# First spectral stage with both column halves behind one left factor, and the sums of a and b formed where they are read

## The chip, the cores and the metric

The kernel runs on one core of a Trainium2 chip. The metric is the device time of one execution in microseconds; the median of three runs before the change is 3003.86 us (2996.85 to 3006.36). One further execution was profiled; its rows are the ones quoted below.

## The reference, cut to what matters

Two independent results stand side by side in the output: attention with 32 heads of 32 columns and one shared key and value head (A), and the real part of a two-dimensional Fourier transform written as products of matrices (B). All arrays are float32.

```python
# A: x is 2048 x 1024, wq 1024 x 1024, wk and wv 1024 x 32, wo 1024 x 1024
q = (x @ wq) in 32 heads of 32 columns;  k = x @ wk;  v = x @ wv
p = softmax(q k^T / sqrt(32));  o = p v;  outA = concat(o) @ wo

# B: x is 2048 x 1024, dft_hid 1024 x 1024, dft_seq 2048 x 2048
a = x @ dft_hid_re^T
b = x @ dft_hid_im^T
outB = dft_seq_re @ a - dft_seq_im @ b

out = concat([outA, outB], axis=-1)      # 2048 x 2048
```

## The kernel before

Every product of matrices that is not part of the attention proper is split in precision: an operand is rounded to a high part, the rest is a low part, and three matmuls (high with high, high with low, low with high) make one product of 128 x 128 by 128 x 512. Such matmuls are called fills here, and their running number is the fill position. They are cut into groups that each fill one 128 x 512 bank (`psb`): a group has one or two left items (`mh`, `ml`: 128 x 512, four blocks of weights) and four or eight right items (`rh`, `rl`: 128 x 512). The order of the groups is a list: first those for k, v and q, then `stage1` (112 groups of 12 fills), then `stage2` (112 groups of 24 fills), then the output projection of A.

The attention runs through the whole kernel in 1024 steps. A step has two matmuls of scores (`pss`), a row maximum on DVE (`nm`), the exponentials on ACT, two matmuls of transposed scores (`pst`) with exponentials into the tile `p`, and every eight steps the matmuls of p and v. `level` hands out the fills in proportion, some five to a step, so that PE alternates between both kinds of work and a stage of the fill list always goes with the same share of attention steps. All five engines keep the order of the program.

How an item gets ready is a line with four steps (`Line`): load, combine, high part, low part, each at a lead in fills ahead of the item's due position; 40, 40, 14 and 8 for right items, 52, 36, 27 and 21 for left items (lines 256 and 257). All DMAs are issued by SP. Combining adds or subtracts several loaded sources on POOL (`comb`, line 210), the high part is a cast on DVE, the low part a subtraction on DVE. A finished left item can be stored and fetched again (`save`, `pre`, `fetch`). The prepared right items sit in 14 buffers, left items in 4.

After a group its `post` runs. If a partial result is to be added, a tile `y` was loaded ahead of time (`load_y`, at most six at once, from 24 fills ahead of the group's end), DVE adds the bank to it, and `store` issues the DMA 9 fills (`BEHIND`) later. Also 9 fills later the six tiles' count is given back (`yused`), and the next `y` may be loaded.

`stage1` forms a and b, both of 2048 x 1024, from x and the two hidden matrices by a scheme of seven products (p1, p2, p6, p7, p5, p3, p4 in this order) instead of eight. The column halves are a pair of real and imaginary blocks (n = 0) and the crosswise pair (n = 1). For each half, for each of the seven products, for each of eight row blocks k there is one group. Partial sums go to memory as `t` and `u2` to `u4`. For n = 0 the left item is made from `xbT`, and its high and low parts are stored in `xb_d`; for n = 1 they are fetched from there. `stage2` multiplies with the sequence matrices (`cT`), again in seven products, whose right operands are single blocks of a and b or sums and differences of two of them. These five sums are formed in `stage1`: where a block is finished whose partner is already in memory, the partner is loaded as one more `y`, POOL adds (`gp.tensor_add` and `gp.tensor_sub` in the `post` of `stage1`), and the sum is stored under the name `r`; single blocks that are needed alone are stored too. `stage2` then loads each right item as one tensor (`right_of`).

Lines that matter: `NR0, NM0, NY` 124, `load_r` 179, `comb` 210, `load_y` 251, `add` with the due positions 262, `take` with `yused` 351 to 373, `stage1` 441, `stage2` 518, `expo` 688, `pv` 698, and the pool `pp` of five tiles `p`, each for two steps. At the start, 28 right items are loaded at once into the not yet used tiles `p` and `h`.

Of the kernel before, what the change touches and what calls it, by code (L numbers as in the profile page):

```python
# [16 lines left out]
P = 128  # L17
# [3 lines left out]
DH = 32  # L21
# [55 lines left out]
class Group:  # L77


    def __init__(self, left, right, post, rows=P, ys=()):  # L80
        self.left, self.right, self.post, self.rows, self.ys = left, right, post, rows, ys
        self.n = 3 * len(right)


@with_exitstack
def tile_kernel(ctx: ExitStack, tc, xT, wq, wkv, wo, xbT, wT, cT, out):
# [19 lines left out]
    xb_d = [[[dram.tile([P, 4, P], F32, name=f"xb_{f}_{k}_{a}") for a in range(2)] for k in range(8)] for f in range(7)]  # L106
# [155 lines left out]
    def add(gs):  # L262

        for g in gs:
            i0 = g.at = end[0]
            end[0] += g.n
            if groups and g.right is not groups[-1].right:
# [83 lines left out]
    def take(n):  # L351
        for _ in range(n):
            if cur["group"] >= len(groups):
                return
            g = groups[cur["group"]]
            j = pos["fill"] - g.at
            if j == 0:
                cur["ps"] = bank("psb", True)
            if j % 3 == 0:
                RL.force(g.right[j // 3])  # L360
            if j % 12 == 0:
                ML.force(g.left[j // 12])
# [12 lines left out]
            run_later()  # L375

# [58 lines left out]
        return Group(left, xs, post)  # L435


    NAMES = {nt: [dram.tile([P, W], F32, name=f"r{i}_{s}") for s in range(NC)] for i, (_, nt, _) in enumerate(PRODUCTS)}
    singles = {k[0]: t for k, t in NAMES.items() if len(k) == 1}

    def stage1():
        done = []
        for n, cols in enumerate((((0, 0), (1, 1)), ((1, 0), (0, 1)))):
            for f, (name, lt, rt, outs) in enumerate(STAGE1):
                keeps = any(t[0] == name for p in STAGE1 for t in p[1] + p[2])

                def x_src(t, k):
                    if isinstance(t[0], str):
                        return (lambda: have(("xr", k), xr_d[k]), t[1])
                    return (lambda: xbT[t[0] * 8 + k, :, t[1] * 4:t[1] * 4 + 4], t[2])  # L450

                def w_src(t, c):
                    if isinstance(t[0], str):
                        return (lambda n=n: have(("wr", n, c), wr_d[n][c]), t[1])
                    r, e = cols[t[0]]
                    return (lambda: wT[r, e, t[1] * 4 + c], t[2])

                R = [Item([w_src(t, c) for t in rt], raw=(wr_d[n][c], ("wr", n, c)) if keeps else None) for c in range(4)]
                for k in range(8):
                    if n:  # L460
                        left = [Item(None, pre=lambda f=f, k=k: have(("xb", f, k), xb_d[f][k]))]
                    else:
                        left = [Item([x_src(t, k) for t in lt], save=(*xb_d[f][k], ("xb", f, k)), raw=(xr_d[k], ("xr", k)) if keeps else None)]
                    ys, plan = [], []
                    for frm, sg, to in outs:
                        it = None
                        if frm is not None:
                            it = Item([(lambda frm=frm, n=n, k=k: have((n, frm, k), u_d[n, frm][k]), 1)])
                            ys.append(it)
                        more = []  # L470
                        if not isinstance(to, str):
                            me = cols[to[1]]
                            s = to[0] * 8 + k
                            for key in NAMES:
                                if len(key) == 2 and me in key:
                                    o = key[0] if key[1] == me else key[1]
                                    if (o, s) in done:
                                        yo = Item([(lambda o=o, s=s: right_of((o,), s), 1)])
                                        ys.append(yo)
                                        more.append((key, yo))  # L480
                            done.append((me, s))
                        plan.append((it, sg, to, more))

                    def post(ps, plan=plan, n=n, k=k, cols=cols):
                        for it, sg, to, more in plan:
# [6 lines left out]
                            if isinstance(to, str):  # L492
                                store(u_d[n, to][k], o, (n, to, k))
                                continue
                            me, s = cols[to[1]], to[0] * 8 + k
# [12 lines left out]
    hs = {}  # L508

    def have(key, ap):  # L510
        assert key in ready, key
        return ap

    def right_of(k, s):
        assert (k, s) in ready
        return NAMES[k][s]

    def stage2():
        seen, total = {}, {}
# [168 lines left out]
    def expo(n):  # L688
        u, r = divmod(n, SU)
        c, hp_ = divmod(r, 2)  # L690
        if hp_ == 0:
            pt[u, c] = pp.tile([P, 4, W], F32, name="p")
        ps = ps_t.tile([P, 2, W], F32, name="pst")
        for a in range(2):
            te.matmul(ps[:, a], kst[:, c * P:(c + 1) * P], qst[u][:, 2 * hp_ + a], start=True, stop=True)
        act.activation(pt[u, c][:, 2 * hp_:2 * hp_ + 2], ps, AF.Exp)

    def pv(u, k):

# [1 line left out]
        ps = bank("psb")  # L701
        for c in range(4 * k, 4 * k + 4):
            for h in range(4):
                te.matmul(ps[h * DH:(h + 1) * DH], v[:, c], pt[u, c][:, h], start=c == 4 * k, stop=c == 4 * k + 3)
        if k == 0:
            ov[u] = onp.tile([P, W], F32, name="ov")
            dve.tensor_copy(ov[u], ps)
# [38 lines left out]
                lse_4(u)  # L746


    room = [(lambda t=t, k=k: t[:, k]) for t in [pp.tile([P, 4, W], F32, name="p") for _ in range(5)] for k in range(4)]
# [109 lines left out]
```

## Time and profile before

| | |
|---|---|
| median of three runs | 3003.86 us (2996.85 to 3006.36) |
| the profiled execution | 2989.74 us, its span 2988.0 us |
| granted TensorE clock, mean | 0.985 |
| PE busy | 2847.3 us, 13904 matmuls |
| DVE busy | 2130.9 us |
| ACT busy | 2246.3 us |
| POOL busy | 584.2 us, 422 instructions |
| DMA | 552.16 MB |

All work is recorded at line 66, since one helper issues every instruction; the rows are told apart by the names of the tiles, output before the arrow and inputs behind it. A stage is found by its tensors: the DMAs of `in_xbT_dram` run from 319.2 to 737.5 us, the first store of `t` starts at 365.3 us, those of `xb` are fetched from 763.7 to 1168.3 us, and the first DMA of `in_cT_dram` (second stage) starts at 1157.0 us. The first spectral stage thus lies between some 355 and 1185 us, the second between 1185 and 2640 us.

### The profile page before, as it was taken

The numbers are of one execution on the slowest core, as the hardware profiler recorded it, in microseconds if no ns is written. First come the engines' busy times: TensorE is split into PE (matmuls) and PEld (weight loads), VectorE is DVE, ScalarE is ACT, GpSimd is POOL, SyncE is SP. The second block draws the span as 40 slices with busy tenths as digits, with TensorE's granted clock in tenths as the row PEclk, the third lists the DMA queues.
The fourth block names the chain that finished last, engine by engine and source line by source line (L and its number), as shares of the span: only waits on it lengthen the run. The fifth ranks groups of instructions, "written<-read, shape, count | busy, mean of one in ns | idle before, by whom it ended". The sixth has DMA issues, their size and how long they took to land.

```text
span 2988.0 us, 40244 instructions
## 1 busy us (share of the span) xinstructions
PE 2847.3 (95%) x13904; PEld 1928.3 (65%) x13904; DVE 2130.9 (71%) x2801; ACT 2246.3 (75%) x3286; POOL 584.2 (20%) x422
## 2 busy tenths in 40 slices
PE   7999998979989888999999999999999999999999
PEld 5767665655656555666666666666666666666656
DVE  6866688867667656778788787788888787865510
ACT  4688887766768666888888887878778788888841
POOL 0000014322141233322221012243232220110000
PEclk9999999989999998999999999999999999999999
DMA  8855579888877788445453244464453442454445
GB/s 292 296 180 159 173 256 312 297 261 264 268 250 254 256 267 279 136 135 166 121 168 121 82 148 132 149 198 141 134 163 116 136 131 75 156 152 138 124 145 162
DMA packets 354892, 552.16 MB, mean 185 GB/s; under 512 B 37760, under 2 KB 102784, under 8 KB 354688
## 3 DMA queue, kind: packets, MB, share of 16 engines
q1 hardware_dynamic: 354688, 549.60, 57.8%
q8 instruction: 109, 1.79, 0.2%
q14 instruction: 95, 0.78, 0.1%
HBM read 393.48 MB, written 154.93 MB: 184 GB/s over the span
## 4 chain that ended last, share of the span: by engine, by line
PE 56%; DVE 7%; DMA 6%; ACT 3%; issue 3%; SPq 1%; POOL 1%; DVEq 0%; ACTq 0%; POOLq 0%
PE psb L66 35%; PE pst L66 11%; PE pss L66 10%; DVE nm L66 3%; DMA r<-y 2%; ACT p L66 2%; ACT pss L66 1%; DMA y<-u 1%; SPq L66 1%; DVE ml L66 1%; DVE rl L66 1%; DVE ov L66 1%; DVE mh L66 1%; POOL m L66 1%; DMA y<-r 0%
## 5 line engine op out<-in xcount | busy, mean ns | idle before, releaser
L66 DVE TENSOR_REDUCE nm<-pss 128x1 f32<-128x1024 f32 x1024 | 1248.5, 1221 | 240.5 <-PE pss L66 237.1
L66 ACT ACTIVATE p<-pst 128x1024 f32<-128x1024 f32 x1024 | 1053.3, 1029 | 387.3 <-PE pst L66 380.8
L66 ACT ACTIVATE pss<-pss,nm 128x1024 f32<-128x1024 f32 x1024 | 1118.1, 1092 | 251.8 <-DVE nm L66 236.7
L66 PE MATMUL psb<-rh,mh 128*128 128x512 f32 (+1 forms) x1852 | 734.5, 397 | 22.5 <-DVE y L66 11.6
L66 PE MATMUL psb<-rh,ml 128*128 128x512 f32 (+1 forms) x1852 | 733.8, 396 | 0.1
L66 PE MATMUL psb<-rl,mh 128*128 128x512 f32 (+1 forms) x1852 | 733.4, 396 | 0.3 <-DVE rl L66 0.3
L66 PE MATMUL pss<-kst,qst 128*128 128x512 f32 x2048 | 665.1, 406 | 55.1 <-ACT pss L66 50.2
L66 PE MATMUL pst<-qst,kst 128*128 128x512 f32 x2048 | 670.0, 408 | 26.6 <-ACT p L66 25.4
L66 PEld LDWEIGHTS pss<-kst,qst 128*128 128x128 f32 x2048 | 371.4, 189 | 258.3 <-issue 92.5
L66 PE MATMUL psb<-p,v 128*32 128x512 f32 x4096 | 476.6, 607 | 23.4 <-DVE y L66 23.3
L66 PEld LDWEIGHTS pst<-qst,kst 128*128 128x128 f32 x2048 | 365.9, 189 | 181.1 <-ACT p L66 107.5
L66 PEld LDWEIGHTS psb<-rh,mh 128*128 128x128 f32 (+1 forms) x1852 | 349.2, 189 | 110.5 <-DVE y L66 13.7
L66 PEld LDWEIGHTS psb<-rl,mh 128*128 128x128 f32 (+1 forms) x1852 | 349.5, 189 | 85.2 <-DVE rl L66 1.8
L66 PEld LDWEIGHTS psb<-rh,ml 128*128 128x128 f32 (+1 forms) x1852 | 349.7, 189 | 84.6 <-issue 0.8
L66 POOL TENSOR_TENSOR m<-m,m 128x512 f32<-128x512 f32 x192 | 264.2, 1382 | 517.5 <-DMA m<-in_cT_dram 379.7
L66 PEld LDWEIGHTS psb<-p,v 128*32 128x32 f32 x4096 | 121.7, 111 | 309.5 <-issue 270.9
L66 DVE TENSOR_TENSOR ov<-ov,psb 128x512 f32<-128x512 f32 x96 | 66.0, 687 | 281.1 <-PE psb L66 281.1
L66 DVE TENSOR_TENSOR ml<-m,mh 128x512 fp32r<-128x512 f32 (+1 forms) x298 | 229.5, 770 | 3.5 <-ACT mh L66 3.1
L66 POOL TENSOR_TENSOR y<-y,h 128x512 f32<-128x512 f32 x64 | 89.9, 1415 | 650.1 <-DVE h L66 575.0
L66 ACT ACTIVATION_READ_ACCUMULATOR pss<-pss,nm 128x1 f32 x1024 | 212.8, 208 | 0.0
L66 DVE CAST mh<-m 128x512 fp32r<-128x512 f32 x291 | 152.3, 523 | 46.6 <-POOL m L66 39.5
L66 DVE TENSOR_TENSOR rl<-r,rh 128x512 fp32r<-128x512 f32 x220 | 176.7, 804 | 4.2 <-ACT rh L66 3.5
(64 smaller groups left out, 837.2 us busy)
## 6 DMA issues: line engine op xcount, KB each, us to landing
m<-in_cT_dram SPq DMA_DIRECT2D x384, 256.0 KB, 3.5
r<-y SPq DMA_DIRECT2D x112, 256.0 KB, 5.2
r<-r SPq DMA_DIRECT2D x112, 256.0 KB, 4.3
y<-y SPq DMA_DIRECT2D x96, 256.0 KB, 4.1
m<-in_xbT_dram SPq DMA_DIRECT2D x80, 256.0 KB, 4.2
y<-u SPq DMA_DIRECT2D x80, 256.0 KB, 3.6
y<-r SPq DMA_DIRECT2D x80, 256.0 KB, 3.3
qst<-qh SPq DMA_DIRECT2D x64, 256.0 KB, 5.7
```

The source lines that it names most:

```text
L66: return lambda *a, **k: self.tc.keep_in_program_order(f(*a, **k))
```

## The change

In `stage1` the loop over the halves n becomes the innermost: a group for n = 0 and the one for n = 1 follow each other with the same left item, and both halves' eight right items are held together. The left item is neither stored nor fetched, and `xb_d` is gone. The blocks of a and b are stored as they are, 64 of them, in `s_d`; no partner is loaded and no sum is made. In `stage2` a right item with two sources loads both, and the add or subtraction is the combine step of its line. For this the second source of a right item gets a tile of its own (two buffers `r1`, where it had one of five tiles `h`), and the tiles `p` become nine of half the size instead of five, so that at the start 26 right items are loaded at once. The due positions of right items are spread over both halves' eight. The count of `y` tiles is given back 18 fills after a group instead of 9.

```diff
         self.n = 3 * len(right)
+
+        self.set, self.first = part or ([right], 0)
...
-            if n == 0:
-                it.t.append(r0p.tile([P, W], F32, name="r0"))
+            if n < 2:
+                it.t.append(r0p.tile([P, W], F32, name=f"r{n}", bufs=NR0 - n))
...
-                    it.due = min(it.need, p0 + (i0 - p0) * (c + 1) // len(g.right))
+                    it.due = min(it.need, p0 + (i0 - p0) * (g.first + c + 1) // (len(g.set) * len(g.right)))
...
-                    soon(lambda n=len(g.ys): yused.__setitem__(0, yused[0] + n))
+                    at(pos["fill"] + 2 * BEHIND, lambda n=len(g.ys): yused.__setitem__(0, yused[0] + n))
...
-        for n, cols in enumerate((((0, 0), (1, 1)), ((1, 0), (0, 1)))):
-            for f, (name, lt, rt, outs) in enumerate(STAGE1):
+        for f, (name, lt, rt, outs) in enumerate(STAGE1):
...
-                R = [Item([w_src(t, c) for t in rt], raw=(wr_d[n][c], ("wr", n, c)) if keeps else None) for c in range(4)]
-                for k in range(8):
-                    if n:
-                        left = [Item(None, pre=lambda f=f, k=k: have(("xb", f, k), xb_d[f][k]))]
-                    else:
-                        left = [Item([x_src(t, k) for t in lt], save=(*xb_d[f][k], ("xb", f, k)), raw=(xr_d[k], ("xr", k)) if keeps else None)]
+            R = [[Item([w_src(t, n, c) for t in rt], raw=(wr_d[n][c], ("wr", n, c)) if keeps else None) for c in range(4)]
+                 for n in range(2)]
+            for k in range(8):
+                left = [Item([x_src(t, k) for t in lt], raw=(xr_d[k], ("xr", k)) if keeps else None)]
+                for n in range(2):
...
-                            if me in singles:
-                                store(singles[me][s], o, ((me,), s))
-                            for key, yo in more:
-                                if key != SUB:
-                                    gp.tensor_add(yo.y, yo.y, o)
-                                elif me == key[0]:
-                                    gp.tensor_sub(yo.y, o, yo.y)
-                                else:
-                                    gp.tensor_sub(yo.y, yo.y, o)
-                                store(NAMES[key][s], yo.y, (key, s))
-                    yield Group(left, R, post, ys=ys)
+                            store(to, o, key)
+                    yield Group(left, R[n], post, ys=ys, part=(R, 4 * n))
...
-                R = [Item([(lambda s=s, nt=nt: right_of(tuple(nt), s), 1)]) for s in range(half * 8, half * 8 + 8)]
+                R = [Item([(lambda s=s, k=k: have((k, s), s_d[k][s]), -1 if nt == SUB and i else 1) for i, k in enumerate(nt)])
+                     for s in range(half * 8, half * 8 + 8)]
...
-    pp = pool(ctx, "pp", 5)
+    pp = pool(ctx, "pp", 9)
...
-        if hp_ == 0:
-            pt[u, c] = pp.tile([P, 4, W], F32, name="p")
+        pt[u, c, hp_] = pp.tile([P, 2, W], F32, name="p")
```

Two places of the order show what moves. The first is the DMA order of SP in the first spectral stage, in product p5, whose groups need two partial sums each. Before, in the half n = 1 (`y` from `u` is a partial sum, `y` from `r` a partner block, `r_…<-y` and `u_…<-y` are stores, `mh` and `ml` from `xb` the left item fetched back):

```order
L66 DMA mh<-xb_7_0_271 128x512
L66 DMA ml<-xb_7_1_272 128x512
L66 DMA u_1_3_380<-y_9401 128x512
L66 DMA r_11_505<-y_9454 128x512
L66 DMA r_11_537<-y_9456 128x512
L66 DMA y_9537<-r_12_522 128x512
L66 DMA y_9539<-r_12_490 128x512
L66 DMA y_9541<-u_1_5_366 128x512
L66 DMA y_9543<-u_1_5_374 128x512
```

And the same product after the change (`m` are the sources of a new left item, which serves two groups; `s_…<-y` stores a finished block):

```order
L66 DMA y_7953<-u_0_5_222 128x512
L66 DMA y_7955<-u_0_5_230 128x512
L66 DMA m_7958<-in_xbT_dram 128x512
L66 DMA m_7960<-in_xbT_dram 128x512
L66 DMA u_0_4_237<-y_7824 128x512
L66 DMA s_12_410<-y_7826 128x512
L66 DMA oh_121<-oh 128x512
L66 DMA ol_125<-ol 128x512
L66 DMA y_8005<-u_1_5_254 128x512
L66 DMA y_8007<-u_1_5_262 128x512
```

Before, a group of p5 has three stores and four loads of `y`, and the loads stand directly behind the stores; now it has two of each, and no `xb` stands between them.

The second place is POOL's order in the fourth product of the second stage, second half, where both a left item with two sources and two sums `y` are formed per group (`h` is the finished product). Before:

```order
L66 TENSOR_TENSOR m_17502<-m_17502,m_17504 128x512
L66 TENSOR_TENSOR y_17517<-y_17517,h_16678 128x512
L66 TENSOR_TENSOR y_17519<-y_17519,h_16678 128x512
L66 TENSOR_TENSOR m_17553<-m_17553,m_17555 128x512
L66 TENSOR_TENSOR m_17601<-m_17601,m_17603 128x512
L66 TENSOR_TENSOR y_17625<-y_17625,h_16802 128x512
L66 TENSOR_TENSOR y_17627<-y_17627,h_16802 128x512
```

After (`r` is the sum of two stored blocks for the next right operand):

```order
L66 TENSOR_TENSOR r_17200<-r_17200,r_17202 128x512
L66 TENSOR_TENSOR m_17150<-m_17150,m_17152 128x512
L66 TENSOR_TENSOR y_17165<-y_17165,h_16300 128x512
L66 TENSOR_TENSOR y_17167<-y_17167,h_16300 128x512
L66 TENSOR_TENSOR m_17205<-m_17205,m_17207 128x512
L66 TENSOR_TENSOR r_17332<-r_17332,r_17334 128x512
L66 TENSOR_TENSOR m_17254<-m_17254,m_17256 128x512
```

One add of `r` per group has come in, and it stands ahead of an add of `m` whose sources SP loads earlier (the numbers rise in the order of the loads: `m_17150` before `r_17200`).

More of the change, by code (lines that the diff above doesn't have):

```diff
@@ L77, with __init__ @@
 class Group:
-    def __init__(self, left, right, post, rows=P, ys=()):
+    def __init__(self, left, right, post, rows=P, ys=(), part=None):
         self.left, self.right, self.post, self.rows, self.ys = left, right, post, rows, ys
         self.n = 3 * len(right)
+        self.set, self.first = part or ([right], 0)
 @with_exitstack
@@ L105, in tile_kernel @@
     wq_d = [[[dram.tile([P, 4, P], F32, name=f"wq_{g}_{q}_{a}") for a in range(2)] for q in range(2)] for g in range(NG)]
-    xb_d = [[[dram.tile([P, 4, P], F32, name=f"xb_{f}_{k}_{a}") for a in range(2)] for k in range(8)] for f in range(7)]
     xr_d = [dram.tile([P, 4, P], F32, name=f"xr_{k}") for k in range(8)]
@@ L266, in add @@
             end[0] += g.n
-            if groups and g.right is not groups[-1].right:
+            if groups and g.set[0] is not groups[-1].set[0]:
                 prev["set"] = prev["this"]
@@ L435, in q_group @@
         return Group(left, xs, post)
-    NAMES = {nt: [dram.tile([P, W], F32, name=f"r{i}_{s}") for s in range(NC)] for i, (_, nt, _) in enumerate(PRODUCTS)}
-    singles = {k[0]: t for k, t in NAMES.items() if len(k) == 1}
+    s_d = {(r, e): [dram.tile([P, W], F32, name=f"s{r}{e}_{s}") for s in range(NC)] for r in range(2) for e in range(2)}
+    COLS = (((0, 0), (1, 1)), ((1, 0), (0, 1)))
     def stage1():
-        done = []
-        for n, cols in enumerate((((0, 0), (1, 1)), ((1, 0), (0, 1)))):
-            for f, (name, lt, rt, outs) in enumerate(STAGE1):
[L445 to L456, printed above, removed]
-                R = [Item([w_src(t, c) for t in rt], raw=(wr_d[n][c], ("wr", n, c)) if keeps else None) for c in range(4)]
-                for k in range(8):
-                    if n:
-                        left = [Item(None, pre=lambda f=f, k=k: have(("xb", f, k), xb_d[f][k]))]
-                    else:
-                        left = [Item([x_src(t, k) for t in lt], save=(*xb_d[f][k], ("xb", f, k)), raw=(xr_d[k], ("xr", k)) if keeps else None)]
@@ new lines, in stage1, with x_src, w_src @@
+        for f, (name, lt, rt, outs) in enumerate(STAGE1):
+            keeps = any(t[0] == name for p in STAGE1 for t in p[1] + p[2])
+            def x_src(t, k):
+                if isinstance(t[0], str):
+                    return (lambda: have(("xr", k), xr_d[k]), t[1])
+                return (lambda: xbT[t[0] * 8 + k, :, t[1] * 4:t[1] * 4 + 4], t[2])
+            def w_src(t, n, c):
+                if isinstance(t[0], str):
+                    return (lambda: have(("wr", n, c), wr_d[n][c]), t[1])
+                r, e = COLS[n][t[0]]
+                return (lambda: wT[r, e, t[1] * 4 + c], t[2])
+            R = [[Item([w_src(t, n, c) for t in rt], raw=(wr_d[n][c], ("wr", n, c)) if keeps else None) for c in range(4)]
[3 more added lines that the diff above has]
+                for n in range(2):
@@ L469, in stage1, with post @@
                             ys.append(it)
[L470 to L485, printed above, removed]
+                        if isinstance(to, str):
+                            plan.append((it, sg, u_d[n, to][k], (n, to, k)))
+                        else:
+                            me, s = COLS[n][to[1]], to[0] * 8 + k
+                            plan.append((it, sg, s_d[me][s], (me, s)))
+                    def post(ps, plan=plan):
+                        for it, sg, to, key in plan:
                             if it is None:
@@ L491, in post @@
                                 (dve.tensor_add if sg > 0 else dve.tensor_sub)(o, o, ps)
[L492 to L495, printed above, removed]
-                            if me in singles:
-                                store(singles[me][s], o, ((me,), s))
-                            for key, yo in more:
-                                if key != SUB:
-                                    gp.tensor_add(yo.y, yo.y, o)
-                                elif me == key[0]:
-                                    gp.tensor_sub(yo.y, o, yo.y)
-                                else:
-                                    gp.tensor_sub(yo.y, yo.y, o)
-                                store(NAMES[key][s], yo.y, (key, s))
-                    yield Group(left, R, post, ys=ys)
+                            store(to, o, key)
+                    yield Group(left, R[n], post, ys=ys, part=(R, 4 * n))
     hs = {}
@@ L512, in have @@
         return ap
-    def right_of(k, s):
-        assert (k, s) in ready
-        return NAMES[k][s]
     def stage2():
@@ L695, in expo @@
             te.matmul(ps[:, a], kst[:, c * P:(c + 1) * P], qst[u][:, 2 * hp_ + a], start=True, stop=True)
-        act.activation(pt[u, c][:, 2 * hp_:2 * hp_ + 2], ps, AF.Exp)
+        act.activation(pt[u, c, hp_], ps, AF.Exp)
     def pv(u, k):
@@ L703, in pv @@
             for h in range(4):
-                te.matmul(ps[h * DH:(h + 1) * DH], v[:, c], pt[u, c][:, h], start=c == 4 * k, stop=c == 4 * k + 3)
+                te.matmul(ps[h * DH:(h + 1) * DH], v[:, c], pt[u, c, h // 2][:, h % 2], start=c == 4 * k, stop=c == 4 * k + 3)
         if k == 0:
@@ L746, in score_step @@
                 lse_4(u)
-    room = [(lambda t=t, k=k: t[:, k]) for t in [pp.tile([P, 4, W], F32, name="p") for _ in range(5)] for k in range(4)]
+    room = [(lambda t=t, k=k: t[:, k]) for t in [pp.tile([P, 2, W], F32, name="p") for _ in range(9)] for k in range(2)]
     room += [(lambda t=t: t) for t in [hp.tile([P, W], F32, name=f"h{k}") for k in range(8)]]
```

## The prediction

> **What bounds the kernel now.** I read the page first, then cut the span into stages, then asked in the worst stage who waits for whom.
>
> ```profile
> PE   7999998979989888999999999999999999999999
> POOL 0000014322141233322221012243232220110000
> DMA  8855579888877788445453244464453442454445
> ```
>
> PE is the busiest engine, and nearly all of its holes lie in slices 7 to 16, where DMA is busy 70 to 90% of the time. The table by stage puts a size to it (columns: PE, PE weight loads, DVE, ACT, POOL busy with counts; granted clock; DMA share; GB/s).
>
> ```profile
> 150.00:355.00 205.00, 203.18 (x1011) 141.62 (x1010) 136.41 (x165) 173.80 (x259) 3.61 (x2) 1.00 0.51 164
> 355.00:1185.00 830.00, 745.93 (x3552) 489.84 (x3554) 583.97 (x759) 587.76 (x857) 229.98 (x166) 0.96 0.82 269
> 1185.00:2640.00 1455.00, 1425.96 (x7137) 967.05 (x7130) 1167.07 (x1553) 1185.63 (x1732) 339.34 (x242) 1.00 0.45 139
> ```
>
> The rows are the q products, the first spectral stage and the second. Fills and attention come in the same proportion in all three, so time per matmul compares them: 205/1011 = 0.2028 us, 830/3552 = 0.2337 us, 1455/7137 = 0.2039 us. At the second stage's rate the first would take 3552 x 0.2039 = 724 us, **106 us less**; at the rate of the q products 720 us, 110 us less. The 106 us have two parts. PE idles 84.1 us instead of 14.5 (29.04 x 3552/7137): 69.6 us. And its busy time per matmul is 0.2100 us instead of 0.1998, with the granted clock at 0.96 instead of 1.00: 36.3 us.
>
> ```profile
> by line: PE psb L66 19.9%; DMA r<-y 7.0%; PE pst L66 6.1%; PE pss L66 5.6%; DMA y<-u 4.9%; SPq L66 3.3%; issue 2.7%; DMA y<-r 1.8%; DVE nm L66 1.4%; ACT p L66 1.2%; DVE y L66 1.2%; DMA y<-t 1.1%; ACT pss L66 0.7%; POOL y L66 0.7%; DMA qst<-
> ...
> DVE y L66 <- DMA y<-u: 47.4, 16, 7.3
> DVE mh L66 <- POOL m L66: 29.4, 9, 8.4
> ...
> DVE y L66 <- DMA y<-t: 8.8, 3, 4.7
> ...
> SPq L66 <- DMA r<-y: 86.1, 71, 5.3
> SPq L66 <- DMA u<-y: 64.8, 21, 6.5
> ```
>
> These are the chain and the waits of that stage alone (355 to 1185 us; total us, times, longest). The chain passes through stores `r<-y`, loads `y<-u`, `y<-r`, `y<-t` and SP's own time for 7.0 + 4.9 + 1.8 + 1.1 + 3.3 = 18.1% of 830 us, some 150 us. DVE, which keeps its order, waits 47.4 + 8.8 us for partial sums and 29.4 us for left items that POOL has not yet combined: 85.6 us, about PE's 84.1 us of idleness. While it waits, the row maxima behind it wait too, then ACT's exponentials, then PE. And the partial sums are late because SP stands 86.1 + 64.8 us before loads whose `y` tile is still being stored: the load is placed directly behind the store.
>
> **The change, part by part.**
>
> ```profile
> r<-y SPq DMA_DIRECT2D x112, 256.0 KB, 5.2
> r<-r SPq DMA_DIRECT2D x112, 256.0 KB, 4.3
> ...
> y<-u SPq DMA_DIRECT2D x80, 256.0 KB, 3.6
> y<-r SPq DMA_DIRECT2D x80, 256.0 KB, 3.3
> ...
> xb<-mh SPq DMA_DIRECT2D x56, 256.0 KB, 3.9
> xb<-ml SPq DMA_DIRECT2D x56, 256.0 KB, 4.2
> mh<-xb SPq DMA_DIRECT2D x56, 256.0 KB, 4.7
> ml<-xb SPq DMA_DIRECT2D x56, 256.0 KB, 5.0
> ```
>
> *Transfers of the first stage.* All 224 transfers of `xb` go. Of 112 stores `r<-y` 64 remain as plain blocks, and the 80 loads `y<-r` go: 224 + 48 + 80 = 352 transfers of 0.262 MB, 92 MB. The stage moves 269 GB/s x 830 us = 223 MB; with 131 MB in some 735 us it would move 178 GB/s, close to the 164 GB/s of the q products, where PE idles 1.8 of 205 us.
>
> *The y tiles.* In p5 for n = 1 a group needs four `y`, so six tiles cover one and a half groups of 12 fills, and the load sits right behind a store that takes 5.2 us to land. Afterwards no group needs more than two; six tiles cover three groups, 36 fills, and the count comes back after 18. In p5 that leaves the load 18 fills or more ahead of its use; at 830 us for 1344 fills (112 groups of 12) a fill takes 0.62 us, so 11 us, against a landing of 3.6 us. The same delay for the second stage costs nothing: its groups have 24 fills, so 24 + 18 fills with two `y` hold at most four tiles of six.
>
> *POOL and the left items.* The 80 adds of partners leave the first stage, where they stood in POOL's order ahead of left sums and waited for DVE. A new left item is due every 24 fills instead of every 12 in the first half and none in the second, so its loads, casts and subtractions spread evenly; DVE's total stays.
>
> ```profile
> L66 DVE TENSOR_TENSOR y<-y,psb 128x512 f32<-128x512 f32 x111 | 74.6, 680 | 79.6 <-DMA y<-u 47.4 <-PE pst L66 9.4 <-DMA y<-t 8.8
> ...
> L66 DVE TENSOR_TENSOR ml<-m,mh 128x512 fp32r<-128x512 f32 x55 | 46.1, 839 | 0.0
> L66 DVE CAST mh<-m 128x512 fp32r<-128x512 f32 x56 | 28.9, 516 | 30.8 <-POOL m L66 29.4 <-DMA m<-in_xbT_dram 1.2
> ```
>
> Per 24 fills DVE then has one left item less than in the second stage (0.52 + 0.84 us) and two additions of `y` more (2 x 0.68 us): the same load, at which it is busy 80% there (1167.07/1455) and PE idles 2.0%.
>
> I take **nine tenths of 106 us, 95 us**. The missing tenth is for the p3, p4, p5 and p6 groups, where two or three sources per left item and right sums still meet two `y` per group.
>
> *The second stage.* It gains 80 loads `r<-s` (21 MB on 202 MB) and 80 adds on POOL with the price of the old ones, 1.37 us:
>
> ```profile
> L66 POOL TENSOR_TENSOR y<-y,y 128x512 f32<-128x512 f32 x80 | 108.6, 1373 | 206.7 <-DVE y L66 127.8 <-DMA y<-r 61.8 <-DMA rb<-r 9.7
> ...
> 1650.00:1725.00 75.00, 74.30 (x371) 51.29 (x364) 57.27 (x82) 62.78 (x94) 0.00 (x0) 1.00 0.22 71
> 1950.00:2025.00 75.00, 70.54 (x344) 47.75 (x343) 67.47 (x81) 58.28 (x85) 33.00 (x24) 1.00 0.65 202
> 2025.00:2100.00 75.00, 73.98 (x379) 49.53 (x378) 58.23 (x81) 61.56 (x92) 20.13 (x15) 1.00 0.46 132
> ```
>
> POOL has room (339 + 110 of 1455 us). But PE's busy time falls from 74.30 us in a stretch without POOL to 70.54 us with 24 of its instructions: 0.157 us each. With 15 of them it falls by 0.32 us, 0.02 each. The new adds come on top of dense phases (five per group in the fourth product, where four stood), so I take the dear end, 80 x 0.157 = **12.5 us**; the cheap end is 80 x 0.02 = 1.7 us, and the costliest is the third rival below. There is no reason for a gain.
>
> Why POOL's density costs DVE time, the rows of the same two stretches show:
>
> ```profile
> L66 DVE TENSOR_TENSOR ml<-m,mh 128x512 fp32r<-128x512 f32 x12 | 8.2, 683 | 0.0
> ...
> L66 DVE TENSOR_TENSOR ml<-m,mh 128x512 fp32r<-128x512 f32 x12 | 11.2, 930 | 0.0
> ```
>
> The subtraction takes 683 ns with POOL still and 930 ns beside it. The Trainium skill ("SBUF — State Buffer", Who interferes with whom) says that DVE with two inputs in SBUF and GpSimd lock each other out for a whole instruction instead of sharing. The trace shows far less than a whole lockout on average, because most instructions do not meet.
>
> *Tiles p and the start.* Nine half tiles hold what the next step of p and v reads (eight) and one being written. No wait comes with it: the matmuls `pst` of the step that reuses a tile stand behind those of p and v on PE, so ACT waits for `pst` anyway.
>
> ```profile
> ACT p L66 <- PE pst L66: 380.8, 277, 5.3
> ...
> p<-in_xT_dram SPq DMA_DIRECT2D x20, 256.0 KB, 5.4
> ```
>
> Two of the 28 early loads come later; hidden behind the first k and v products I cost them at nothing, and fully exposed they would be 2 x 5.4 = 11 us.
>
> *Sum.* -95 + 12.5 = -83 us, so the profiled execution's 2989.74 us would be 2907 us. The runs' median is 14 us above that execution; I carry the difference over unchanged: 3003.86 - 83 = **2921 us**.
>
> **The rivals.**
>
> 1. *The waits only halve.* SP still stands before loads behind stores, and the left items of p6 to p4 still meet right sums on POOL. For it: 28.2 of DVE's 29.4 us for left items fall in the half whose pattern (new left items) now fills the stage. Against it: they come at half the rate. Half of 106 us minus 12.5 us is 40 us: 2963 us.
>
> ```profile
> PE pss L66 <- ACT pss L66: 50.2, 40, 5.1
> PE psb L66 <- DVE y L66: 35.8, 11, 9.7
> ```
>
> The Trainium skill ("TensorE: Matmul & The Clock Gate", What's actually happening) halves the array's clock after about 3.4 us of idleness and gives it back after as long of work. The waits here reach 5.1 and 9.7 us, and the clock is 0.96, which agrees; by that rule waits cut below 3.4 us would return all of the 36 us, and this rival would end at 3003.86 - 36 - 35 + 12.5 = 2945 us.
>
> 2. *Nothing is won*: the transfers saved were beside the path, and DVE's order sets the stage at any DMA load. For it, DVE is in every chain of waits; against it, the second stage has the same DVE load and idles 2.0%. 3004 us.
>
> 3. *Slower, by POOL's order.* In the second stage each new add of `r` stands ahead of an add of `m` and waits for a younger load. In the first half this has happened already:
>
> ```profile
> L66 POOL TENSOR_TENSOR r<-r,h 128x512 f32<-128x512 f32 x20 | 27.7, 1387 | 224.8 <-DMA h<-in_wT_dram 182.2 <-DMA r<-wr 16.8 <-DVE rl L66 9.7
> ...
> DVE mh L66 <- POOL m L66: 28.2, 8, 8.4
> ...
> DVE mh L66 <- POOL m L66: 10.0, 8, 2.5
> ```
>
> In 365 to 770 us POOL waited 182.2 us before 20 such adds, and DVE 28.2 us for left items: 1.41 us per add. Eighty of them cost 113 us: -95 + 12.5 + 113 = +31 us, 3034 us. It decides from (95 - 12.5)/80 = 1.03 us per add. Against it: SP in the second stage is far less loaded (0.45 against 0.82), and DVE waits there for left items only 10.0 us in all (third row, 1185 to 2640 us). A right load is due 26 fills (14 us) before its cast and lands in 4.3 us.
>
> 4. *Slower, by the lockout.* Every new add blocks DVE for its whole 1.37 us: 110 us instead of 12.5, -95 + 110 = +15 us, 3019 us. The two `ml` rows speak against it, at 0.25 us per subtraction. The rule of the Trainium skill cited above ("SBUF — State Buffer", Who interferes with whom), taken at its worst, is this case.
>
> **How the numbers follow.** Forecast 0.72, its own range 2896 to 2950 (from -110 + 1.7 us to eight tenths of 106 us with twice the price, -85 + 25 us, and some runs' spread). Rival 1: 0.16. Rival 2: 0.04. Rival 3: 0.05. Rival 4: 0.03. The range 2896 to 2970 holds most of the forecast and of the first rival, about 0.8. About 0.3%, 9 us, is what a measurement can tell from no change; forecast and rival 1 are faster by more (0.88), rival 2 is the same (0.04), rivals 3 and 4 are slower (0.08).
>
> **What would show it.** Right: the first stage takes 725 to 745 us at a granted clock of 0.99 or more and below 200 GB/s; DVE's waits for `y<-u` and `y<-t` nearly vanish; total transfers fall by 272 x 0.262 = 71 MB to 481 MB; the second stage grows by some 12 us, where POOL is densest. Wrong: SP's waits before `y` loads stay above 100 us and DVE still waits for `y` (rival 1), the stage is freed of transfers but keeps 0.23 us per matmul (rival 2), DVE waits for POOL's `m` or `r` in the second stage by more than 30 us (rival 3), or its subtractions there go to 1.2 us and more on average (rival 4).

## The result and the profile after

The changed kernel takes 2885.49 us (median of four runs, 2884.68 to 2886.87) against 3000.36 us before in the same comparison (2991.97 to 3006.36): a ratio of 0.962, 95% interval 0.9593 to 0.9646, 115 us less. The forecast was 2921 us with a range of 2896 to 2970: the direction was right, and the gain was larger than the range allowed.

The profiled execution took 2884.95 us, with a span of 2883.0 us. These are the lines of its page that answer to those shown of before:

```profile
PE   8999999999999999999999999999999999999999
POOL 0000001332111113222331022452443420210000
DMA  8855425665566455454453344564554533454445
```

The holes of PE in slices 7 to 16 are closed, and DMA there stands at 40 to 70%. POOL's work has moved to the right.

To compare stages exactly, both traces are cut at the same work: the ends of the 129th, 257th, 417th and 897th row maximum (the DVE rows `nm` in order of time), since both kernels have the same 1024 of them. The second and third piece are the two halves of the first spectral stage with the first few groups of the second stage, the fourth is second stage alone. The first block is before, the second after (columns as in the prediction):

```profile
0.00:376.50 376.50, 359.16 (x1668) 255.23 (x1669) 265.66 (x347) 273.37 (x424) 9.61 (x11) 0.99 0.67 221
376.50:760.80 384.30, 344.17 (x1647) 224.11 (x1646) 299.47 (x401) 271.46 (x395) 111.11 (x78) 0.97 0.84 277
760.80:1241.60 480.80, 434.27 (x2064) 287.66 (x2063) 310.13 (x392) 340.78 (x497) 137.87 (x102) 0.95 0.78 252
1241.60:2502.20 1260.60, 1235.18 (x6179) 838.07 (x6178) 1017.84 (x1350) 1029.91 (x1505) 297.50 (x212) 1.00 0.45 138
```

```profile
0.00:381.50 381.50, 361.38 (x1668) 258.12 (x1669) 266.74 (x350) 273.34 (x424) 9.62 (x11) 0.98 0.64 212
381.50:714.80 333.30, 329.03 (x1650) 223.63 (x1649) 256.67 (x335) 274.25 (x403) 73.10 (x54) 1.00 0.55 184
714.80:1133.00 418.20, 412.11 (x2061) 279.27 (x2060) 340.35 (x454) 337.00 (x489) 80.92 (x60) 1.00 0.58 190
1133.00:2398.80 1265.80, 1237.85 (x6178) 836.08 (x6177) 1035.29 (x1349) 1029.45 (x1504) 385.61 (x277) 1.00 0.48 151
```

The matmul counts agree to a few, so the stretches hold the same work. The first half of the stage fell from 384.3 to 333.3 us (51.0 less), the second from 480.8 to 418.2 us (62.6 less), the second stage grew from 1260.6 to 1265.8 us (5.2 more), the start by 5.0 us, and what is left at the end fell by 1.6 us. The sum is -105.0 us, the difference of the two spans.

Who waits for whom on DVE and SP in the first spectral stage after the change (381.5 to 1133 us):

```profile
DVE ov L66 <- PE psb L66: 89.0, 34, 4.0
DVE nm L66 <- PE pss L66: 56.9, 105, 1.8
DVE y L66 <- PE psb L66: 5.4, 12, 1.3
DVE rh L66 <- PE psb L66: 0.4, 1, 0.4
...
SPq L66 <- DVE y L66: 231.5, 81, 10.5
...
SPq L66 <- DMA u<-y: 29.0, 13, 4.2
```

In this stage DVE now waits for PE alone; not one wait for a partial sum or a left item is left. SP waits only 29.0 us for the stores `u<-y` (86.1 us for `r<-y` and 64.8 us for `u<-y` in the rows of the prediction). It also waits 231.5 us for DVE's additions, but no load is late by that: DVE waits for none.

### The profile page after: what moved, and what is told of

It reads as the page before. It is cut to its first block, busy times and chain, and to the rows that moved or that the text cites. A ratio compares the mean times of both kernels' runs of the same rounds, so it can differ in the third digit from the quotient of the medians.

```text
span 2883.0 us, 39659 instructions
## 1 busy us (share of the span) xinstructions
PE 2814.2 (98%) x13904; PEld 1919.1 (67%) x13904; DVE 2137.8 (74%) x2801; ACT 2244.9 (78%) x3286; POOL 580.2 (20%) x422
## 2 busy tenths in 40 slices
DMA packets 315719, 480.80 MB, mean 167 GB/s; under 512 B 33408, under 2 KB 98432, under 8 KB 315520
## 4 chain that ended last, share of the span: by engine, by line
PE 78%; DVE 11%; ACT 5%; issue 3%; DMA 2%; POOL 1%; SPq 1%; ACTq 0%; POOLq 0%; DVEq 0%
PE psb L66 50%; PE pst L66 15%; PE pss L66 14%; DVE nm L66 4%; ACT p L66 3%; ACT pss L66 2%; DVE rl L66 1%; DVE ml L66 1%; DMA r<-s 1%; DVE ov L66 1%; DVE mh L66 1%; SPq L66 1%; DVE rh L66 1%; POOL m L66 0%; POOL y L66 0%
## 5 line engine op out<-in xcount | busy, mean ns | idle before, releaser
L66 PE MATMUL psb<-p,v 128*32 128x512 f32 x4096 | 466.0, 595 | 0.5 <-DVE y L66 0.5
L66 POOL TENSOR_TENSOR r<-r,r 128x512 f32<-128x512 f32 x112 | 147.7, 1319 | 824.5 <-DMA r<-s 403.5
```

The lines of the kernel that those rows point to most:

```text
L66: return lambda *a, **k: self.tc.keep_in_program_order(f(*a, **k))
```

## The experiments

The kernels were timed in three batches, each batch on one chip and in turns with the kernel before. The stages are cut as above, at each kernel's own 129th, 257th and 417th row maximum; these columns come from one profiled execution each. That execution can lie off the median: 10 us below it for the kernel with eight y and the partner adds left out, 9 us above it for the one with the partner adds left out.

| run | median us | ratio to before, 95% interval | half 1, us | half 2, us |
|---|---|---|---|---|
| before (four medians) | 2998 to 3003 | 1 | 384.3 | 480.8 |
| sums moved, loop order of before | 2919.85 | 0.9732 (0.9717 to 0.9748) | 365.9 | 414.6 |
| the same with y after 18 | 2916.18 | 0.9722 (0.9706 to 0.9738) | 362.2 | 417.9 |
| after, with y after 9 | 2884.38 | 0.9614 (0.9596 to 0.9631) | 335.0 | 416.6 |
| after, 224 transfers put back | 2890.60 | 0.9636 (0.9621 to 0.9651) | 337.5 | 416.9 |
| after | 2885.49 | 0.9620 (0.9593 to 0.9646) | 333.3 | 418.2 |
| after, left item not shared | 2917.05 | 0.9710 (0.9693 to 0.9726) | 349.2 | 437.2 |
| the same, and stored | 2937.19 | 0.9796 (0.9779 to 0.9813) | 362.7 | 443.2 |
| before with eight y | 2954.67 | 0.9842 (0.9827 to 0.9856) | 359.4 | 463.1 |
| before, partner adds left out | 2976.82 | 0.9931 (0.9906 to 0.9955) | 391.7 | 465.9 |
| eight y, partner adds left out | 2920.31 | 0.9733 (0.9709 to 0.9756) | 356.7 | 429.8 |

**The parts of the change.** The sums were moved, with the halves still in the outer loop and the left items stored and fetched; then the same with the later return of the y count; and the changed kernel was run with the early return.

The first has the half tiles `p`, the tiles `r1` and the 26 early loads of the changed kernel, and keeps the loops and left items of before. In its `stage1` the loads of partners are gone, and the end of `post` is

```diff
-                            if me in singles:
-                                store(singles[me][s], o, ((me,), s))
-                            for key, yo in more:
...
+                            store(to, o, key)
...
```

and the third is the changed kernel with

```diff
-                    at(pos["fill"] + 2 * BEHIND, lambda n=len(g.ys): yused.__setitem__(0, yused[0] + n))
+                    soon(lambda n=len(g.ys): yused.__setitem__(0, yused[0] + n))
```

> The sums of a and b move to the second stage as in the change, but the halves stay in the outer loop, the left items are stored and fetched (224 transfers) and the y count comes back after 9 fills. Theory T (stage 1 waits because of the sheer number of transfers, so the gain goes by their share, 128 of 352): the first stage gets about 41 us faster, 2960 us in all. Theory Y (it waits because up to four y tiles per group are loaded directly behind stores, and because POOL's adds of partners stand ahead of the left sums): nearly the whole gain of the stage, 80 to 110 us, comes with this part alone, 2895 to 2925 us, and PE idles little in the second half, where DVE waited 56 us for y.

> As the run with the sums moved alone, but with the y count coming back after 18 fills. Theory T: the same time as without it, within 5 us. Theory Y: 5 to 15 us faster than without it, since in p5 the load no longer stands behind a store that has not landed.

> The changed kernel with the y count coming back after 9 fills again. Theory T: the same as the changed kernel, 2885 us, within 4 us. Theory Y: 5 to 15 us slower, 2890 to 2900 us, with DVE waits for y<-u again in p5.

Moving the sums brought 0.9732, some 79 of the 115 us, just at the edge of what theory Y expected; with it came the whole gain of the second half and a third of that of the first. The loop order brought the rest, all in the first half: with the early return of the y count from 365.9 to 335.0 us, with the late one from 362.2 to 333.3 us, that is 31 and 29 us (by the medians 35 and 31 us). The later return of the y count brought nothing that can be measured, either with the old loop order (0.9722 against 0.9732) or with the new one (0.9614 without it, 0.9620 with it): here theory Y was wrong. The later return alone, in the kernel before, was not tried.

**Transfers alone.** The changed kernel stores the left items again and loads them into tiles that nobody reads:

```diff
-                left = [Item([x_src(t, k) for t in lt], raw=(xr_d[k], ("xr", k)) if keeps else None)]
+                left = [Item([x_src(t, k) for t in lt], save=(*xb_d[f][k], ("xb", f, k)), raw=(xr_d[k], ("xr", k)) if keeps else None)]
...
+                        if n:
+                            for a in have(("xb", f, k), xb_d[f][k]):
+                                sp.dma_start(spare(0, 5).rearrange("p (a b) -> p a b", a=4), a)
```

> The changed kernel with 224 transfers put back that do nothing: the left items' parts are stored as before (112), and for the second half of each pair two loads of them go into tiles that nobody reads (112). Theory T: 224 of 352 transfers bring back 64% of the 114 us, some 73 us, 2958 us. Theory Y: within 10 us of the changed kernel, at most 2895 us, though the stage's DMA rate goes from 187 GB/s to about 265 GB/s.

The table by stage of this kernel, its two halves:

```profile
380.50:718.00 337.50, 330.75 (x1650) 223.44 (x1650) 259.49 (x336) 274.37 (x403) 75.02 (x54) 1.00 0.78 261
718.00:1134.90 416.90, 411.14 (x2065) 280.79 (x2064) 339.36 (x454) 337.58 (x489) 82.03 (x60) 1.00 0.80 263
```

DMA is about as busy as before the change (0.78 and 0.80 against 0.84 and 0.78; 261 and 263 GB/s against 277 and 252), and PE is still busy 98% of the time at the full clock. The median is 5 us longer, not 73. Theory T fell: a DMA share of 0.8 does not by itself make this stage wait. The loads put back have no reader, so this run says nothing of a load that something waits for.

**The left items.** Each of the two groups of a pair made its own left item; then both of its parts were stored too.

```diff
-                left = [Item([x_src(t, k) for t in lt], raw=(xr_d[k], ("xr", k)) if keeps else None)]
                 for n in range(2):
+                    left = [Item([x_src(t, k) for t in lt], raw=(xr_d[k], ("xr", k)) if keeps and n == 0 else None)]
```

and in the second run of the two

```diff
-                    left = [Item([x_src(t, k) for t in lt], raw=(xr_d[k], ("xr", k)) if keeps and n == 0 else None)]
+                    left = [Item([x_src(t, k) for t in lt], save=xb_d[n][f][k], raw=(xr_d[k], ("xr", k)) if keeps and n == 0 else None)]
```

> The changed kernel, but each of the two groups of a pair makes its own left item: 56 items more are loaded, combined and cast (about 56 x (0.42 + 0.68) = 62 us more on DVE and 40 adds more on POOL), one every 12 fills through the whole stage, and no item is stored or fetched. Theory L (what the loop order saved is the rate of left items in the first half: one every 12 fills keeps POOL and DVE late): the second half of the stage now loses what the first half had lost, 2 x 30 us, 2935 to 2955 us, with DVE waiting for POOL's left sums. Theory O (the saving came from the order itself, from transfers or from the groups' neighbourhood): within 10 us of the changed kernel, at most 2895 us.

> The kernel in which each group makes its own left item (2917 us), with both parts of each left item stored too, as the half n = 0 did before: 224 stores that nobody reads, one pair every 12 fills. If the stores at that rate are the rest of what the first half lost: 16 us per half, 2945 to 2950 us. If stores cost what they cost at half the rate (5 us for 224 transfers): 2922 us.

A left item for every 12 fills cost 16 us in the first half (333.3 to 349.2) and 19 us in the second, half of what theory L expected for each. The stretches and DVE's wait for left items in this kernel:

```profile
377.60:726.80 349.20, 336.07 (x1651) 223.45 (x1651) 292.04 (x386) 275.06 (x403) 103.90 (x75) 1.00 0.66 210
726.80:1164.00 437.20, 419.88 (x2061) 279.97 (x2060) 377.64 (x509) 336.90 (x488) 105.94 (x78) 0.99 0.67 210
...
DVE mh L66 <- POOL m L66: 10.6, 4, 7.7
```

DVE is busy 84 and 86% of the two halves instead of 77 and 81%, 73 us more in all, and waits for POOL's left sums only 10.6 us. This speaks for DVE's own time as the larger part and POOL's lateness, which theory L had named too, as the smaller, but no run separates the two. The stores then cost 13.5 us more in the first half and 6.0 us in the second; both expectations for them missed, 2937 us lies between 2922 and 2945. With them the first half takes 362.7 us, what it took with the old loop order and the same late return of the y count (362.2). The loop order's 29 us are thus the rate of left items (16 us) and their stores at that rate (13.5 us).

**The y tiles and POOL's adds of partners.** Three runs on the kernel before: two more `y` tiles; the 80 adds left out; both.

```diff
-    NR0, NM0, NY = 3, 3, 6
+    NR0, NM0, NY = 3, 3, 8
...
-    pp = pool(ctx, "pp", 5)
+    pp = pool(ctx, "pp", 9)
...
```

```diff
-                                if key != SUB:
-                                    gp.tensor_add(yo.y, yo.y, o)
-                                elif me == key[0]:
-                                    gp.tensor_sub(yo.y, o, yo.y)
-                                else:
-                                    gp.tensor_sub(yo.y, yo.y, o)
```

> The kernel before with eight y tiles instead of six (the room comes from nine half tiles p instead of five whole ones); all transfers, sums and the loop order as before. Theory Y (in the half n = 1 the loads of y stand directly behind stores because four per group share six tiles): the second half gets 25 to 45 us faster, 2955 to 2975 us, and SP's waits for r<-y and u<-y fall by half. Theory P (it is POOL's adds of partners, or the mere number of transfers): at most 8 us, 2990 us or more.

> The kernel before with its 80 adds and subtractions of partners on POOL left out; the partners are still loaded into y tiles and stored (unsummed), so the transfers and the number of y tiles stay. Theory A (POOL's adds in the first stage matter by themselves: they stand ahead of the left sums, lock out DVE and hold y tiles longer): 20 to 40 us faster than before, 2960 to 2980 us. Theory Y (only the scarcity of y tiles): within 8 us of before, 2992 us or more.

> The kernel before with eight y tiles (2955 us) and the 80 adds of partners left out. If tiles and adds are two separate costs: 20 to 35 us less than with eight tiles alone, 2920 to 2935 us. If eight tiles cure what the adds did: within 6 us of 2955 us. What is left then up to 2916 us is the 128 transfers of partners.

The kernels without the adds store the partners unsummed. Eight tiles gave 49 us, more than theory Y expected, and not in the second half alone: by the two traces 24.9 us in the first, 17.7 us in the second. In the first half DVE's wait for left items fell with them from 28.2 to 11.7 us, although POOL's work was the same. The room for the two tiles comes from the half tiles `p`, whose effect alone was not run; before, ACT waited to write `p` for `pst` alone, so no wait for a tile `p` shows that they could have cured. SP's waits in that kernel's stage (378.6 to 1201.1 us):

```profile
SPq L66 <- POOL y L66: 55.7, 22, 6.2
...
SPq L66 <- DMA r<-y: 36.4, 30, 3.6
...
SPq L66 <- DMA u<-y: 12.4, 12, 4.5
```

The waits for stores fell from 88.0 + 64.8 us in the same piece of before to 36.4 + 12.4 us. What stays is SP's wait for POOL's adds (54.6 us before): the store of a sum stands in SP's order until POOL has formed it. Without the adds (and with eight tiles) another 34 us go, to 2920.31 us; by the traces 33.3 of 36.0 us in the second half. There SP's wait goes, but also DVE's waits become shorter (in the stage for `y<-u` from 31.8 to 18.0 us, for left items from 25.1 to 10.9 us), and DVE's busy time falls by 10 us; no run separates these three. With six tiles the adds alone are worth 22 us by the medians: the two costs are not independent.

2920.31 us is also the time of the kernel with the sums moved, 2919.85 us, but the two are equal by luck, and it does not follow that the 128 partner transfers are free. That kernel still forms the 80 sums, in the second stage, and has six tiles. Its second half, and below it that of the kernel with eight tiles and no adds:

```profile
746.00:1160.60 414.60, 410.19 (x2065) 281.07 (x2064) 305.99 (x391) 340.06 (x497) 68.27 (x50) 1.00 0.71 227
...
733.40:1163.20 429.80, 414.74 (x2061) 280.81 (x2060) 302.40 (x391) 340.57 (x497) 49.74 (x36) 0.99 0.84 275
...
DVE y L66 <- DMA y<-u: 18.0, 8, 5.4
```

With the partners still loaded and stored, the second half is 15.2 us longer and DVE waits 18.0 us in it for partial sums (last row), where the kernel with the sums moved shows no such wait. Its first half is 9.2 us shorter, and its second stage 8.6 us shorter (1261.0 against 1269.6 us). So the moved sums' 79 us are some 49 us for the scarcity of `y` tiles, some 34 us for the adds and a part for the partner transfers, which no run measures alone (the 15.2 us are the nearest), less what the sums cost in the second stage.

**The second stage and the start.** One source left out; 28 early loads again; the sum of right items formed later.

```diff
-                R = [Item([(lambda s=s, k=k: have((k, s), s_d[k][s]), -1 if nt == SUB and i else 1) for i, k in enumerate(nt)])
+                R = [Item([(lambda s=s, k=k: have((k, s), s_d[k][s]), -1 if nt == SUB and i else 1) for i, k in enumerate(nt[:1])])
```

```diff
+    room += [lambda: r0p.tile([P, W], F32, name="r0", bufs=NR0) for _ in range(2)]
```

```diff
-    RL = Line(NR0, NR, (40, 40, 14, 8), load_r, comb, hi_r, lo)
+    RL = Line(NR0, NR, (40, 28, 14, 8), load_r, comb, hi_r, lo)
```

> The changed kernel with only the first of the two blocks read as right item of the second stage; the second block's 80 loads and the 80 adds or subtractions on POOL are left out. If the moved adds cost what the prediction said (12.5 us in the second stage), 2873 us; by the aligned traces (5.5 us), 2880 us.

> The changed kernel with 28 right items loaded at the start again, the two more into the staging tiles r0. If the two later loads made the start 3 to 5 us later, 2881 us and the 32nd row maximum at the time of before; if not, 2885 us within 1.5 us.

> The changed kernel with the combine step of right items 28 fills ahead instead of 40, behind the left sums whose sources are loaded earlier. Leaving the sums out altogether gives 2875.5 us, so that is the most. If the order on POOL costs anything in the second stage: 2878 to 2882 us; if it is the lockout and DVE's time alone: 2885 us within 2 us.

Without the second source, which leaves out a part of the product, the time is 2875.51 us (0.9578, 0.9564 to 0.9593), 10 us less. The second stage of this kernel, cut like the fourth piece above:

```profile
1130.90:2391.30 1260.40, 1236.50 (x6180) 840.38 (x6179) 1014.69 (x1349) 1031.28 (x1505) 297.96 (x212) 1.00 0.46 138
```

It takes 1260.4 us, what it took before (1260.6), so against the changed kernel's trace the moved adds cost 5.4 us; the medians say 10 us for both stages. The other traces put it in between: this piece took 1260.3 to 1262.1 us in the five kernels without the moved adds and 1265.8 to 1270.4 us in the nine with them, 7.5 us more on average. DVE's busy time is 20.6 us less than with them (1014.69 against 1035.29) for 65 adds in this stretch (277 - 212 instructions): 0.32 us per add. The Trainium skill ("SBUF — State Buffer", Who interferes with whom) has a DVE instruction with two inputs in SBUF and one of GpSimd lock each other out for the whole instruction; the full 1.37 us for each add does not show here.

With 28 early loads the time is 2885.65 us (0.9615, 0.9600 to 0.9629): no change. With the sum formed later it is 2883.61 us (0.9622, 0.9601 to 0.9644): no change either. No version that forms all sums beats the changed kernel clearly. The start's 5 us in the two traces are not explained by the two late loads: with them early again the 32nd row maximum ends at 138.4 us (135.5 before, 140.3 after), and the kernel with its left items not shared, which has the same start as the changed one, reaches the 129th at 377.6 us, 1.1 us after the one before. The start scatters between traces by as much.

## Why the prediction was wrong

The place, the direction and the chain of causes were right; the sizes of three terms were not, and most of the error lies in the first of them.

*What bounds the kernel.* Right: PE's holes were in the first spectral stage, DVE waited there for partial sums and left items, and SP stood before loads behind stores. DVE's waits named went to zero, and SP's fell from 150.9 to 29.0 us. PE's waits, of which the prediction shows 50.2 and 35.8 us, are now

```profile
PE pss L66 <- ACT pss L66: 18.1, 20, 3.9
...
PE psb L66 <- DVE y L66: 0.5, 1, 0.5
```

over the whole execution. One reading of the prediction is too wide: the chain that it quotes reaches back only to 681 us, so its 150 us of stores, loads and SP's time lie in the last 504 us of the stage, not in all 830.

*"I take nine tenths of 106 us, 95 us."* This step failed, by 18.6 us: the two halves lost 113.6 us. Some 11 of the 18.6 us are the tenth that was held back, and no row had given it a price: the stage, with the p3 to p6 groups for which it was kept, shows no wait of DVE for a source any more. The rest is that the 106 us were no ceiling. They set the second stage's pace, 0.2039 us per matmul, as the best that the first could reach. The first now takes 751.5 us for 3711 matmuls, 0.2025 us, the pace of the q products (0.2028), by which the prediction had 110 us and did not take it. PE is busy 98.6% of it (741.1 of 751.5 us) against 97.8% of the second stage. Why the second stage is slower stays open: POOL is busy there 385.6 of 1265.8 us after the change, but 154.0 of 751.5 us in the first; yet the q products, with 3.6 of 205 us, are no faster than the first.

*The second stage's 12.5 us.* Too dear: 5.2 us in the two traces, 7.5 us over all traces with and without the moved adds, 10 us by the medians. The price per instruction came from the one densest stretch; the average add meets less.

*The median carried over unchanged.* This cost 10 us: the profiled execution before, 2989.74 us, lies below all timed runs of its kernel (2992 to 3006 us), and the one after, 2884.95 us, is at its median. The offset was that of one execution, and the prediction carried it over as if it were the kernel's. Runs of the kernel before scatter by 5 to 14 us in the four comparisons, those of the changed one by 2 us and of three of its variants (y after 9, 28 early loads, the sum formed later) by 5 to 7 us; that the removed waits took scatter with them is likely, not shown.

The parts add up: 18.6 us from the first stage, 7.3 us from the second, 10 us from the offset, 1.6 us at the end, less the start's 5.0 us, make the 32 us between the forecast gain of 83 us and the measured 115 us.

*The transfers.* They were listed first among the causes, and their fall to 480.80 MB was forecast right (481). But 224 of them put back cost 5 us. What counted was less how many bytes moved than what stood behind what: loads behind stores for want of `y` tiles (49 us), POOL's adds and what waited for them (34 us), and left items and their stores at twice the pace (30 us). The partner transfers, which do stand in this order, keep a share that was not measured alone. The y count's return after 18 fills, to which the prediction gave a paragraph, changed nothing.

*The rivals.* The first, waits that only halve, was refuted by DVE's list of waits. Its sentence on the clock cannot be judged, since the long waits went altogether; the granted clock is 1.00 in both halves of the stage now, and of the 113.6 us some 37 are PE's shorter busy time (778.4 to 741.1 us). The second, that nothing is won, fell with the result. The third, POOL's order in the second stage, fell too: DVE waits there for left items 7.5 us in all after the change (1076 to 2540 us), 10.0 us before.

```profile
DVE mh L66 <- POOL m L66: 7.5, 7, 1.3
```

The fourth, the lockout, fell as well: the subtractions `ml` of the second stage take 796 ns on average after the change and 772 ns before, not 1.2 us.

## What to carry to other kernels

A busy DMA beside a waiting engine is not yet a cause: ask which instruction stands in front of the late load in the issuing queue, and for which buffer or engine it waits; adding buffers or taking away that one instruction tells more than counting bytes. When waits are removed from one stage, the pace of a neighbouring stage is not its floor; here the fastest stretch on record, the q products, gave the pace that was reached, and a tenth held back without a price was lost. And before a time from one execution is carried over to a median, look at the scatter of the runs. Two kernels that take the same time need not do so for the same reason: cut them by stage.

## What the runs showed of the hardware that was not expected

The 16 DMA engines at a mean share of 0.8 and some 262 GB/s left PE busy 98% of the time in the first spectral stage of the changed kernel; the dead transfers' whole price was 5 us for 224 of them. Adds on POOL also held up SP: with eight tiles and the adds in place SP waited 55.7 us in the stage for POOL's results, although POOL was busy less than a third of the time (245.2 of 822.5 us), because in SP's order the store of each sum stands ahead of every later load. And only a part of DVE's instructions took longer beside POOL: from the stretch of the prediction without POOL (1650 to 1725 us) to the one with 24 of its instructions (1950 to 2025 us) the cast `mh` went from 419 to 757 ns and the subtraction `ml` from 683 to 930 ns, while the row maximum `nm`, which reads a bank, took 1223 and 1218 ns.
